# Full-row score products, and first-group weight conversion on one buffer without GpSimd, in an attention, expert and dense kernel

## The chip, the cores and the metric

One NeuronCore of a Trainium2 chip runs the whole program in one launch. The metric is device microseconds of that core, the median of several executions. A second number is the span, from the first to the last instruction of one profiled execution.

## The reference, cut to what matters

Three layers run one after the other, all in fp32.

```
scores = q @ k^T / 8, causal; a = softmax(scores); local = a @ v         # B, H, S, D = 4, 8, 576, 64
q_p = phi(q);  mem = (q_p @ M_prev) / (q_p . z_prev + 1e-6)
x = g * mem + (1 - g) * local                                            # 2304 tokens x 512
e = argmax(x @ w_gate);  x = gate * eom * relu(x @ w1[e]) @ w2[e]        # 8 experts, 1024 wide
h = relu(x @ w_in);  out = (h * h) @ w_out                               # dense, 2048 wide, weights given as float64
```

## The kernel before, in words

An fp32 product is made of three fp32r products (`mm3`): each operand is split into a high part that fp32r holds exactly and the rest, and high x high, high x low and low x high are summed in PSUM.

**Attention.** The 32 heads are worked as 16 pairs; the two heads of a pair lie on partitions 0 to 63 and 64 to 127. Each pair goes through four stages (prep, front, back, end), and in one round of the loop four neighbouring pairs are each in another stage; `PLAN` says how their steps are interleaved, and a scheduler at compile time then fixes the order of every engine's queue. In prep, ScalarE and VectorE split q and k into `qh`, `ql`, `kh`, `kl`, and SyncE (SP) issues eight DMAs that stack `kh` over `kl` and `qh` twice (`k2`, `q2`, L201 and L202), so that one product over 128 rows gives high x high and high x low of one head. In front, `scores` makes for each head the stacked product, then the product `ql` x `kh` over the 64 rows of this head alone (L229 both), and then a bf16 product that adds the causal mask (L239); the three calls cover 512, 256 + 128 and 384 columns. The last 64 query rows go another way (`psl`, full rows). In back, the weights are transposed into `aT` and multiplied with v (L332): four blocks of 128 key rows, and a fifth block of only 64 rows. v and the k and q of later pairs are loaded by SP as well; the load of v (L209) is the first DMA of a round in SP's queue and waits for the product of an earlier pair that read the same buffer.

**Experts.** Routed tokens run through their expert, in an order of ScalarE's, VectorE's, GpSimd's and TensorE's instructions that is written out by hand. Into this order two of the dense weight conversions (f = 0 and 1) and the first y transposes are put (`dense_prep`, `AH`).

**Dense.** Five groups of up to 512 tokens; each runs over 16 slices f of the hidden width: `l1` (12 products, L81 to L83 on `phf`), relu, square, split into `gT`, then `l2` (12 products on `po`), one f behind `l1`. During the first group the weights of slice f + 2 are converted from float64, whose bits are put together again with integer operations: for each of the two matrices (512 columns each) ScalarE takes the absolute value (L1089), VectorE runs four operations (L1091, L1093, L1096, L1098), ScalarE copies the high part (L1100) and GpSimd subtracts for the low part (L1102). GpSimd also makes the low part of `gT` in this group (L1168); in the others VectorE does. The later groups find the weights converted.

Of the kernel before, what the change touches and what calls it, by code (L numbers as in the profile page):

```python
# [33 lines left out]
GW = P + 32  # L34
NRAW = 3
AH = ((3, 0), (3, 2), (3, 2), (3, 2), (3, 2), (2, 0), (2, 2), (2, 2), (1, 1), (1, 1))
# [6 lines left out]
XG = 4  # L43
XF = 2
NP = 6
# [18 lines left out]
WARM = 11  # L64
MASK_LAST = True
TK = 3
# [69 lines left out]
def attention(tc, c, q, k, v, x_dram, pools):  # L136
# [9 lines left out]
    pvs = [lt.tile([P, SP_], F32, name=f"pvs{i}") if i else per.tile([P, SP_], F32, name=f"pvs{i}") for i in range(2)]  # L146
    qlast = [[per.tile([P, P], F32R, name=f"qlast{t}{i}") for t in "hl"] for i in range(2)]
    for i in range(3):
        nc.gpsimd.memset(qpad[i][:, S:], 0.0)
    for i in range(2):  # L150
        nc.gpsimd.memset(pvs[i][:, S:], 0.0)
        for t in range(2):
            nc.gpsimd.memset(qlast[i][t].bitcast(F32), 0.0)
    c.setup()
    c.lg = c.pool.tile([P, NCOL, 2 * E], F32, name="lg")
# [5 lines left out]
    def pair(b, hp, lgT):  # L161
# [18 lines left out]
        yield  # L180
        qh = fr.tile([P, S], F32R, tag="qh", name="qh")
        ql = fr.tile([P, S], F32R, tag="ql", name="ql")
        ex = fr.tile([P, S], F32, tag="ex", name="ex", bufs=1)
# [4 lines left out]
        nc.vector.scalar_tensor_tensor(out=ql, in0=qs, scalar=0.125, in1=qh.bitcast(F32), op0=ALU.mult, op1=ALU.subtract)  # L188
        for t, src in enumerate((qh, ql)):
            for h in range(2):  # L190
                r = slice(64 * h, 64 * h + 64)
                early.tensor_copy(qlast[i][t][r, r], src[r, 512:S].bitcast(F32))
# [14 lines left out]

        vt = ld.tile([P, NB, 2, D], F32, tag="vraw", name="vraw", bufs=2)
        nc.sync.dma_start(out=vt[:, 0:4].rearrange("p c h d -> p c (h d)"), in_=v[b, hp, 0:512].rearrange("(c p) d -> p c d", p=P))  # L209
# [7 lines left out]
        def scores(js):  # L217
            banks = [bank(f"sc{js[0]}{h}") for h in range(2)]
            off = [sum((i + 1) * P for i in js[:t]) for t in range(len(js))]
            o, n = off[-1] + js[-1] * P, len(js)  # L220
            mask = c.maskd.unsqueeze(1).to_broadcast((P, n, P))
            for h in range(2):
                r = slice(64 * h, 64 * h + 64)

                def product(qx, kx, start, stop):
                    for i, j in enumerate(js):
                        nk = (j + 1) * P
                        lhs, rhs = (qx[:, h], kx[:, h]) if len(qx.shape) == 3 else (qx[r], kx[r])
# [10 lines left out]
                nc.tensor.matmul(banks[h][:, o - (n - 1) * P:o + P], lhsT=c.identb, rhs=mask, start=False, stop=MASK_LAST)  # L239
                if not MASK_LAST:  # L240
                    product(ql, kh, False, True)
# [25 lines left out]

        aT = at.tile([P, 2, 1664], F32, tag="aT", name="aT", bufs=2)
        ko = (0, 576, 1024, 1344, 1536)
# [57 lines left out]
        for kb in range(NB):  # L327
            kn = P if kb < 4 else LAST
# [736 lines left out]
def dense_prep(tc, c, st, w_in, w_out):  # L1065
# [3 lines left out]
    cv = e(tc.tile_pool(name="cv", bufs=2, side="right", reuse_waits="tile"))  # L1069
    thr = 2.0 ** -15 * (1.0 + 0.125)  # L1070
    win32 = w_in.bitcast(I32).rearrange("(k p) (f t) -> p k f t", p=P, t=2)
# [4 lines left out]
    def weights(f, pool):  # L1076
        c.wi[f] = pool.tile([P, 2, 4, P], F32R, name=f"wi{f}")
        c.wo[f] = pool.tile([P, 2, DM], F32R, name=f"wo{f}")
        dst = [c.wi[f].rearrange("p t k f -> p t (k f)"), c.wo[f]]
        src = [win32[:, :, f * P:(f + 1) * P, :], wout32[f * P:(f + 1) * P]]  # L1080
        raw, u, x = ([cv.tile([P, 512] + [2] * (nm == "fraw"), dt, tag=nm, name=nm, bufs=nb) for _ in range(2)]
                     for nm, dt, nb in (("fraw", I32, NRAW), ("u", I32, 2), ("x", F32, XF)))
        for i in range(2):
            with tc.issue_after(c.last) if f < NPRE else nullcontext():
                nc.sync.dma_start(out=raw[i] if i else raw[i].rearrange("p (k f) t -> p k f t", k=4), in_=src[i])
        yield
        lw, hw = ([r[:, :, t] for r in raw] for t in range(2))
        for i in range(2):
            nc.scalar.activation(x[i], hw[i].bitcast(F32), AF.Abs)  # L1089
        for i in range(2):  # L1090
            nc.vector.tensor_scalar(out=u[i], in0=hw[i], scalar1=0x07FFFFFF, scalar2=3, op0=ALU.bitwise_and, op1=ALU.logical_shift_left)  # L1091
        for i in range(2):
            nc.vector.scalar_tensor_tensor(out=u[i], in0=lw[i], scalar=29, in1=u[i], op0=ALU.logical_shift_right, op1=ALU.bitwise_or)  # L1093
        yield
        for i in range(2):
            nc.vector.scalar_tensor_tensor(out=u[i], in0=hw[i], scalar=-1073741824, in1=u[i], op0=ALU.bitwise_and, op1=ALU.bitwise_or)  # L1096
        for i in range(2):
            nc.vector.scalar_tensor_tensor(out=x[i], in0=x[i], scalar=thr, in1=u[i].bitcast(F32), op0=ALU.is_ge, op1=ALU.mult)  # L1098
        for i in range(2):
            nc.scalar.copy(dst[i][:, 0], x[i])  # L1100
        for i in range(2):
            c.psub = nc.gpsimd.tensor_sub(dst[i][:, 1], x[i], dst[i][:, 0].bitcast(F32))  # L1102
        yield
# [3 lines left out]
    yT = c.yT[0] = c.yTeven()  # L1107
    yt = [cv.tile([P, 2, DM], F32, tag="fraw", name="ytp", bufs=NRAW) for _ in range(2)]
    for j in range(2):
        with tc.issue_after(c.last):  # L1110
            nc.sync.dma_start(out=yt[j], in_=c.y_first[2 * j * P:(2 * j + 2) * P].rearrange("(i p) f -> p i f", p=P))
    yield
    for j in range(4):
        turn(nc, c, c.bank("pty"), yt[j // 2][:, j % 2], yT[:, :, j])
        if j % 2:
            yield
# [13 lines left out]
def dense(tc, c, st, out):  # L1130
# [25 lines left out]
    def l1(g, f):  # L1156
# [20 lines left out]
    for g, (b0, nb) in enumerate(groups):  # L1177
# [23 lines left out]
        if g < len(groups) - 1:  # L1201
            l2(g, NF - 1, gts.pop(NF - 1), po, range(nb))
        else:
# [111 lines left out]
```

## Time and profile before

| | before |
|---|---|
| device time, median of 3 runs | 974.2 us (973.51 to 974.49) |
| the profiled execution's own time | 973.51 us |
| its span | 971.8 us |
| TensorE busy in the span | 930.1 us (96%) |
| VectorE, ScalarE, GpSimd busy | 599.5, 468.7, 246.4 us |
| mean granted clock of TensorE | 0.986 |

A busy TensorE is not one at its peak: the end of a matmul is modelled, and a start that is late because the array was not ready counts as busy too. What a product really costs is read from the distance between the starts of neighbours.

### The profile page before, as it was taken

Reading aid. Unit: us, or ns where it says so; the run is one execution under the profiler, and the core shown is the slowest. Engines: PE = TensorE matmul, PEld = TensorE weight load, DVE = VectorE, ACT = ScalarE, POOL = GpSimd, SP = SyncE. Lnnn points to the kernel's source line nnn. Section 1 sums busy time; section 2 is a strip of 40 time slices with the busy share of each in tenths; the row PEclk is TensorE's granted clock in tenths of the full one; section 3 lists DMA queues with packets and bytes.
Section 4 is the critical chain, followed back from the end, with each engine's and each line's share of the span. In section 5 each row is a group of like instructions: output and inputs, shape, how many; then the busy total and the mean of one; then the engine's idle time right before and its main releaser. Section 6 shows DMA issues by size and latency. Waiting matters only on the chain. (4 is left out here: it accounts for less than half of the span.)

```text
span 971.8 us, 14590 instructions
## 1 busy us (share of the span) xinstructions
PE 930.1 (96%) x5212; PEld 735.4 (76%) x5212; DVE 599.5 (62%) x1142; ACT 468.7 (48%) x950; POOL 246.4 (25%) x301
## 2 busy tenths in 40 slices
PE   7999999999999999999999787799999999999996
PEld 4676676776566889889898565678888888888895
DVE  6677878778486887767678899943223222322232
ACT  6877777774445666565563444442222222322231
POOL 6233233231201033054322555562001100100010
PEclk8999999999999999999999999899999999999999
DMA  9675575552746978765735444431000100100000
GB/s 194 168 173 144 145 174 147 131 136 84 236 140 209 377 263 306 258 230 198 272 111 166 136 132 131 130 87 65 12 11 33 33 1 0 44 1 1 12 33 22
DMA packets 80923, 125.03 MB, mean 129 GB/s; under 512 B 8848, under 2 KB 35472, under 8 KB 80848
## 3 DMA queue, kind: packets, MB, share of 16 engines
q1 hardware_dynamic: 76224, 109.11, 37.1%
q0 software_dynamic: 4624, 14.95, 4.8%
q8 instruction: 43, 0.70, 0.3%
q14 instruction: 32, 0.26, 0.1%
HBM read 109.10 MB, written 15.99 MB: 129 GB/s over the span
## 5 line engine op out<-in xcount | busy, mean ns | idle before, releaser
L1165 DVE SCALAR_TENSOR_TENSOR r<-phf,r 128x512 f32<-128x512 f32 (+1 forms) x80 | 50.9, 636 | 178.9 <-ACT r L1164 178.9
L81 PE MATMUL phf<-yT,wi 128*128 128x512 f32 (+1 forms) x320 | 123.3, 385 | 19.2 <-DVE r L1165 19.2
L1164 ACT ACTIVATE r<-phf 128x512 f32<-128x512 f32 (+1 forms) x80 | 44.4, 555 | 177.9 <-PE phf L83 163.0
L848 DVE TENSOR_TENSOR wc<-raw,wc 128x1024 fp32r<-128x1024 f32 x91 | 117.3, 1331 | 12.0 <-ACT wc L846 10.3
L83 PE MATMUL phf<-yT,wi 128*128 128x512 f32 (+1 forms) x320 | 120.1, 375 | 0.0
L82 PE MATMUL phf<-yT,wi 128*128 128x512 f32 (+1 forms) x320 | 119.9, 375 | 0.0
L846 ACT CAST wc<-raw 128x1024 fp32r<-128x1024 f32 x108 | 106.5, 1056 | 20.0 <-DMA raw<-in_w_dram 14.8
L81 PE MATMUL po<-wo,gT 128*128 128x512 f32 x256 | 101.6, 398 | 1.5 <-ACT gT L1167 1.5
L82 PE MATMUL po<-wo,gT 128*128 128x512 f32 x256 | 101.0, 395 | 0.0
L83 PE MATMUL po<-wo,gT 128*128 128x512 f32 x256 | 89.0, 390 | 0.0
L81 PEld LDWEIGHTS phf<-yT,wi 128*128 128x128 f32 x320 | 61.2, 191 | 35.6 <-DVE r L1165 18.6
L244 DVE TENSOR_REDUCE negm<-sc 128x1 f32<-128x512 f32 (+3 forms) x128 | 59.0, 483 | 30.6 <-PE sc L239 28.6
L247 ACT ACTIVATE a<-sc,negm 128x512 f32<-128x512 f32 (+3 forms) x128 | 67.1, 529 | 21.5 <-DVE negm L244 20.7
L81 PE MATMUL py<-wc,hT 128*128 128x512 f32 x176 | 69.9, 397 | 0.7 <-ACT hT L885 0.7
L82 PE MATMUL py<-wc,hT 128*128 128x512 f32 x176 | 68.8, 391 | 0.8 <-DVE wc L848 0.8
L83 PEld LDWEIGHTS phf<-yT,wi 128*128 128x128 f32 x320 | 61.3, 192 | 10.8
L83 PE MATMUL py<-wc,hT 128*128 128x512 f32 x176 | 68.9, 391 | 0.3 <-DVE hT L886 0.3
L82 PEld LDWEIGHTS phf<-yT,wi 128*128 128x128 f32 x320 | 61.5, 192 | 10.0
L848 POOL TENSOR_TENSOR wc<-raw,wc 128x1024 fp32r<-128x1024 f32 x17 | 45.2, 2658 | 91.6 <-ACT wc L846 83.9
L1212 POOL DMA_INDIRECT out_dram<-ob,rtok x13 | 12.9, 991 | 204.7 <-DVE ob L1211 179.6
L1167 ACT CAST gT<-r 128x512 fp32r<-128x512 f32 x64 | 39.8, 621 | 45.4 <-DVE r L1165 37.0
L81 PEld LDWEIGHTS po<-wo,gT 128*128 128x128 f32 x256 | 49.3, 193 | 12.9 <-ACT gT L1167 2.2
(338 smaller groups left out, 2092.5 us busy)
## 6 DMA issues: line engine op xcount, KB each, us to landing
raw<-in_w_dram SPq DMA_DIRECT2D x64, 1024.0 KB, 6.7
fraw<-in_w_in_dram SPq DMA_DIRECT2D x16, 512.0 KB, 4.0
fraw<-in_w_out_dram SPq DMA_DIRECT2D x16, 512.0 KB, 3.7
q<-qh SPq DMA_DIRECT2D x60, 128.0 KB, 2.5
kraw<-in_k_dram SPq DMA_DIRECT2D x16, 288.0 KB, 5.3
qraw<-in_q_dram SPq DMA_DIRECT2D x16, 288.0 KB, 3.2
y_rest<-y SPq DMA_DIRECT2D x17, 256.0 KB, 3.0
vraw<-in_v_dram SPq DMA_DIRECT2D x16, 256.0 KB, 3.1
```

Of the source, the lines that this page charges most:

```text
L81: nc.tensor.matmul(out, lhsT=lh, rhs=rh, start=start, stop=False)
L82: nc.tensor.matmul(out, lhsT=lh, rhs=rl, start=False, stop=False)
L83: return nc.tensor.matmul(out, lhsT=ll, rhs=rh, start=False, stop=stop)
L244: nc.vector.tensor_reduce(out=negm[:, h, j:j + 1], in_=psv, axis=AX.X, op=ALU.max, negate=True)
L247: nc.scalar.activation(a[:, h, aoff[j]:aoff[j] + nk], psv, AF.Exp, bias=negm[:, h, j:j + 1], accum_out=ssum[:, h, j:j + 1])
L846: nc.scalar.copy(wc[:, 0, ks], raw[:, ks])
L848: eng.tensor_sub(wc[:, 1, ks], raw[:, ks], wc[:, 0, ks].bitcast(F32))
L1164: nc.scalar.activation(r[:, 0:nt], ph[:, 0:nt], AF.Relu)
L1165: nc.vector.scalar_tensor_tensor(out=r[:, 0:nt], in0=ph[:, 0:nt], scalar=0.0, in1=r[:, 0:nt], op0=ALU.max, op1=ALU.mult)
L1167: nc.scalar.copy(gT[:, 0, 0:nt], r[:, 0:nt])
L1212: nc.gpsimd.indirect_dma_start(out=out, out_offset=bass.IndirectOffsetOnAxis(ap=c.tok[b0 + j], axis=0), in_=ob, in_offset=None)
```

## The change

It has two parts that do not touch each other.

In attention, `ql` x `kh` becomes a product over all 128 rows: `ql` is carried by two more DMAs into a buffer `qlz` whose other 64 rows are zero for each head, and the partner is `kh` of both heads. The fifth block of the product with v takes 128 rows too; the buffers of v and `aT` become permanent, with zeros in the rows that are not used. `qh` and `ql` have one buffer in place of two.

In the dense part, both matrices of a slice are converted by one operation of each kind over 1024 columns, in place in one buffer `x`: absolute value, a maximum with a small number, three integer operations, the copy of the high part, and the subtraction, now on VectorE. The square in the first group moves from VectorE to ScalarE, the low part of `gT` from GpSimd to VectorE, and `l2` runs two f behind `l1` in this group.

```diff
-NRAW = 3
+NRAW = 2
-XF = 2
+XF = 1
...
+    qlz = [per.tile([P, 2, 512], F32R, name=f"qlz{i}") for i in range(2)]
+    vts = [per.tile([P, NB, 2, D], F32, name=f"vts{i}") for i in range(2)]
+    aTs = [per.tile([P, 2, 1664], F32, name=f"aTs{i}") for i in range(2)]
...
+        for h in range(2):
+            nc.gpsimd.memset(qlz[i][64 - 64 * h:128 - 64 * h, h].bitcast(F32), 0.0)
+        nc.gpsimd.memset(vts[i][LAST:P, 4], 0.0)
+        nc.gpsimd.memset(aTs[i][LAST:P, :, 1536:1600], 0.0)
...
-        qh = fr.tile([P, S], F32R, tag="qh", name="qh")
-        ql = fr.tile([P, S], F32R, tag="ql", name="ql")
+        qh = fr.tile([P, S], F32R, tag="qh", name="qh", bufs=1)
+        ql = fr.tile([P, S], F32R, tag="ql", name="ql", bufs=1)
...
-        for t, src in enumerate((qh, ql)):
-            for h in range(2):
-                r = slice(64 * h, 64 * h + 64)
+        for h in range(2):
+            r = slice(64 * h, 64 * h + 64)
+            nc.sync.dma_start(out=qlz[i][r, h].bitcast(F32), in_=ql[r, 0:512].bitcast(F32))
+            for t, src in enumerate((qh, ql)):
                 early.tensor_copy(qlast[i][t][r, r], src[r, 512:S].bitcast(F32))
...
-                if MASK_LAST:
-                    product(ql, kh, False, False)
+                for i_, j in enumerate(js):
+                    nk = (j + 1) * P
+                    nc.tensor.matmul(banks[h][:, off[i_]:off[i_] + nk], lhsT=qlz[i][:, h, j * P:nk], rhs=kh[:, 0:nk], start=False, stop=False)
...
-                nc.tensor.matmul(pa[o, q0 - P:448], lhsT=vt[0:kn, kb, h, :], rhs=aT[0:kn, h, ko[kb] + q0 - kb * P:ko[kb] + S - kb * P],
+                nc.tensor.matmul(pa[o, q0 - P:448], lhsT=vt[:, kb, h, :], rhs=aT[:, h, ko[kb] + q0 - kb * P:ko[kb] + S - kb * P],
...
+        raw = cv.tile([P, 2, 512, 2], I32, tag="fraw", name="fraw", bufs=NRAW)
+        x = cv.tile([P, 1024], I32, tag="x", name="x", bufs=XF)
+        xf = x.bitcast(F32)
...
+        nc.scalar.activation(xf, hw.bitcast(F32), AF.Abs)
+        nc.vector.tensor_scalar_max(xf, xf, tiny)
+        nc.vector.tensor_scalar(out=x, in0=x, scalar1=0x07FFFFFF, scalar2=3, op0=ALU.bitwise_and, op1=ALU.logical_shift_left)
+        nc.vector.scalar_tensor_tensor(out=x, in0=lw, scalar=29, in1=x, op0=ALU.logical_shift_right, op1=ALU.bitwise_or)
+        nc.vector.scalar_tensor_tensor(out=x, in0=hw, scalar=-1073741824, in1=x, op0=ALU.bitwise_and, op1=ALU.bitwise_or)
+        nc.scalar.copy(hi, xf)
         yield
...
-            c.psub = nc.gpsimd.tensor_sub(dst[i][:, 1], x[i], dst[i][:, 0].bitcast(F32))
+        c.psub = nc.vector.tensor_sub(lo, xf, hi.bitcast(F32))
...
-        nc.vector.scalar_tensor_tensor(out=r[:, 0:nt], in0=ph[:, 0:nt], scalar=0.0, in1=r[:, 0:nt], op0=ALU.max, op1=ALU.mult)
-        gT = dg.tile([P, 2, 512], F32R, tag="gT", name="gT", bufs=2) if g < len(groups) - 1 else c.gring[:, f % 8]
+        if g:
+            nc.vector.scalar_tensor_tensor(out=r[:, 0:nt], in0=ph[:, 0:nt], scalar=0.0, in1=r[:, 0:nt], op0=ALU.max, op1=ALU.mult)
+        else:
+            nc.scalar.activation(r[:, 0:nt], r[:, 0:nt], AF.Square)
+        gT = dg.tile([P, 2, 512], F32R, tag="gT", name="gT", bufs=3) if g < len(groups) - 1 else c.gring[:, f % 8]
...
-        (nc.vector if g else nc.gpsimd).tensor_sub(gT[:, 1, 0:nt], r[:, 0:nt], gT[:, 0, 0:nt].bitcast(F32))
+        nc.vector.tensor_sub(gT[:, 1, 0:nt], r[:, 0:nt], gT[:, 0, 0:nt].bitcast(F32))
...
+        lag = 1 if g else 2
...
-                if f >= 1:
-                    l2(g, f - 1, gts.pop(f - 1), po, range(nb))
+                if f >= lag:
+                    l2(g, f - lag, gts.pop(f - lag), po, range(nb))
```

## Rows read from the trace of the kernel before

**Rows 1.** Busy time in two stretches: length, each engine's us, TensorE clock, DMA share.

```profile
50.00:200.00 150.00, 150.00 (x1109) 107.00 (x1108) 116.58 (x329) 112.44 (x324) 47.58 (x96) 1.00 0.62 153
...
600.00:610.00 10.00, 6.12 (x25) 4.81 (x26) 10.00 (x13) 4.59 (x8) 5.31 (x4) 0.97 0.49 149
```

**Rows 2.** TensorE in order of time, one round of attention: start us, us, instruction.

```profile
108.36 0.29 PE L82 MATMUL psl<-kl,qlasth 128*128 128x288 f32 x1
108.49 0.29 PE L83 MATMUL psl<-kh,qlastl 128*128 128x288 f32 x1
...
110.19 0.49 PE L229 MATMUL sc<-kh,ql 64*128 64x512 f32 x1
110.61 0.23 PE L239 MATMUL sc<-maskd,identb 128*128 128x128 bf16 x1
110.65 0.48 PE L229 MATMUL sc<-k,q 128*128 128x512 f32 x1
111.06 0.50 PE L229 MATMUL sc<-kh,ql 64*128 64x512 f32 x1
```

**Rows 3.** Weight loads by form, 50 to 200 us: count, busy, mean ns, idle before.

```profile
L229 PEld LDWEIGHTS sc<-k,q 128*128 128x128 f32 x82 | 14.3, 193 | 0.7 <-issue 0.3
L229 PEld LDWEIGHTS sc<-kh,ql 64*128 64x128 f32 x82 | 13.6, 183 | 10.8 <-issue 9.2
...
L239 PEld LDWEIGHTS <-identb 128*128 128x128 bf16 x62 | 5.9, 95 | 10.3 <-issue 8.7
...
L332 PEld LDWEIGHTS pva<-aT,vraw 64*64 64x64 f32 x40 | 2.3, 131 | 2.5 <-issue 2.5
```

**Rows 4.** SP's queue in order of time, one round.

```profile
105.09 0.38 SPq L209 DMA_DIRECT2D vraw<-in_v_dram  x1
...
114.86 0.45 SPq L170 DMA_DIRECT2D kraw<-in_k_dram  x1
120.55 0.38 SPq L209 DMA_DIRECT2D vraw<-in_v_dram  x1
```

**Rows 5.** The start: GpSimd and TensorE in order of time.

```profile
6.65 0.41 POOL L156 MEMSET lg<- 128x320 f32 x1
...
11.77 0.23 PE L239 MATMUL sc<-maskd,identb 128*128 128x128 bf16 x1
17.85 1.11 PE L77 MATMUL ptl<-ident,al 128*128 128x128 f32 x4 [5.86 <-ACT al L257]
```

**Rows 6.** VectorE in order of time, first dense group, f = 2 and f = 11.

```profile
552.61 0.68 DVE L1165 SCALAR_TENSOR_TENSOR r<-phf,r 128x512 f32<-128x512 f32 x1
...
624.88 0.68 DVE L1165 SCALAR_TENSOR_TENSOR r<-phf,r 128x512 f32<-128x512 f32 x1
```

**Rows 7.** Single lines: ns shortest/median/longest, first and last start us, form.

```profile
L1091 DVE TENSOR_SCALAR u<-fraw x32: 411/417/1515, 499.3 to 632.1; 128x512 int32<-128x512 int32 x32
L1093 DVE SCALAR_TENSOR_TENSOR u<-fraw,u x32: 676/679/1785, 500.6 to 633.0; 128x512 int32<-128x512 int32 x32
L848 DVE TENSOR_TENSOR wc<-raw,wc x91: 1204/1217/3435, 261.5 to 516.1; 128x1024 fp32r<-128x1024 f32 x91
L846 ACT CAST wc<-raw x108: 1029/1054/1098, 260.4 to 515.6; 128x1024 fp32r<-128x1024 f32 x108
L1102 POOL TENSOR_TENSOR wo<-x,wo x16: 1277/1348/1747, 509.2 to 639.6; 128x512 fp32r<-128x512 f32 x16
```

**Rows 8.** A later dense group in order of time: TensorE, ScalarE, VectorE.

```profile
802.40 0.39 PE L81 MATMUL phf<-yT,wi 128*128 128x512 f32 x1
...
805.12 0.39 PE L81 MATMUL phf<-yT,wi 128*128 128x512 f32 x1
...
804.64 0.60 ACT L1164 ACTIVATE r<-phf 128x512 f32<-128x512 f32 x1 [3.62 <-PE phf L83]
...
805.27 0.69 DVE L1165 SCALAR_TENSOR_TENSOR r<-phf,r 128x512 f32<-128x512 f32 x1 [3.52 <-ACT r L1164]
```

**Rows 9.** Both ends of the first dense group in order of time: ScalarE, TensorE.

```profile
536.58 0.61 ACT L1100 CAST wi<-x 128x512 fp32r<-128x512 f32 x1
...
639.78 0.50 PE L81 MATMUL phf<-yT,wi 128*128 128x512 f32 x1
```

More of the change, by code (lines that the diff above doesn't have):

```diff
@@ L64 @@
 WARM = 11
-MASK_LAST = True
 TK = 3
@@ L206, in pair @@
         yield "prep"
-        vt = ld.tile([P, NB, 2, D], F32, tag="vraw", name="vraw", bufs=2)
+        vt = vts[i]
         nc.sync.dma_start(out=vt[:, 0:4].rearrange("p c h d -> p c (h d)"), in_=v[b, hp, 0:512].rearrange("(c p) d -> p c d", p=P))
@@ L236, in scores @@
                     product(qh, kl, False, False)
-                if MASK_LAST:
-                    product(ql, kh, False, False)
-                nc.tensor.matmul(banks[h][:, o - (n - 1) * P:o + P], lhsT=c.identb, rhs=mask, start=False, stop=MASK_LAST)
-                if not MASK_LAST:
-                    product(ql, kh, False, True)
+                for i_, j in enumerate(js):
+                    nk = (j + 1) * P
+                    nc.tensor.matmul(banks[h][:, off[i_]:off[i_] + nk], lhsT=qlz[i][:, h, j * P:nk], rhs=kh[:, 0:nk], start=False, stop=False)
+                nc.tensor.matmul(banks[h][:, o - (n - 1) * P:o + P], lhsT=c.identb, rhs=mask, start=False, stop=True)
             views = [(banks[h][:, off[i]:off[i] + (j + 1) * P], h, j) for i, j in enumerate(js) for h in range(2)]
@@ L266, in pair @@
         yield "front"
-        aT = at.tile([P, 2, 1664], F32, tag="aT", name="aT", bufs=2)
+        aT = aTs[i]
         ko = (0, 576, 1024, 1344, 1536)
@@ L327, in pair @@
         for kb in range(NB):
-            kn = P if kb < 4 else LAST
             q0 = max(P, kb * P)
@@ L1069, in dense_prep @@
     cv = e(tc.tile_pool(name="cv", bufs=2, side="right", reuse_waits="tile"))
-    thr = 2.0 ** -15 * (1.0 + 0.125)
+    tiny = 2.0 ** -15
     win32 = w_in.bitcast(I32).rearrange("(k p) (f t) -> p k f t", p=P, t=2)
@@ L1076, in weights @@
     def weights(f, pool):
[L1077 to L1082, printed above, removed]
@@ L1083, in weights @@
-        for i in range(2):
-            with tc.issue_after(c.last) if f < NPRE else nullcontext():
-                nc.sync.dma_start(out=raw[i] if i else raw[i].rearrange("p (k f) t -> p k f t", k=4), in_=src[i])
-        yield
[L1087 to L1091, printed above, removed]
@@ L1092, in weights @@
-        for i in range(2):
-            nc.vector.scalar_tensor_tensor(out=u[i], in0=lw[i], scalar=29, in1=u[i], op0=ALU.logical_shift_right, op1=ALU.bitwise_or)
-        yield
[L1095 to L1100, printed above, removed]
@@ L1101, in weights @@
-        for i in range(2):
-            c.psub = nc.gpsimd.tensor_sub(dst[i][:, 1], x[i], dst[i][:, 0].bitcast(F32))
+        w = pool.tile([P, 2, 2, 512], F32R, name=f"w{f}")
+        c.wi[f] = w[:, :, 0].rearrange("p t (k q) -> p t k q", k=4)
+        c.wo[f] = w[:, :, 1]
+        hi, lo = (w[:, t].rearrange("p i q -> p (i q)") for t in range(2))
+        raw = cv.tile([P, 2, 512, 2], I32, tag="fraw", name="fraw", bufs=NRAW)
+        x = cv.tile([P, 1024], I32, tag="x", name="x", bufs=XF)
+        xf = x.bitcast(F32)
@@ new lines, in weights @@
+        with tc.issue_after(c.last) if f < NPRE else nullcontext():
+            nc.sync.dma_start(out=raw[:, 0].rearrange("p (k f) t -> p k f t", k=4), in_=win32[:, :, f * P:(f + 1) * P, :])
+            nc.sync.dma_start(out=raw[:, 1], in_=wout32[f * P:(f + 1) * P])
+        yield
+        lw, hw = (raw.rearrange("p i q t -> p (i q) t")[:, :, t] for t in range(2))
+        nc.scalar.activation(xf, hw.bitcast(F32), AF.Abs)
+        nc.vector.tensor_scalar_max(xf, xf, tiny)
+        nc.vector.tensor_scalar(out=x, in0=x, scalar1=0x07FFFFFF, scalar2=3, op0=ALU.bitwise_and, op1=ALU.logical_shift_left)
@@ L1107, in dense_prep @@
     yT = c.yT[0] = c.yTeven()
-    yt = [cv.tile([P, 2, DM], F32, tag="fraw", name="ytp", bufs=NRAW) for _ in range(2)]
+    yt = cv.tile([P, 4, DM], F32, tag="fraw", name="ytp", bufs=NRAW)
     for j in range(2):
         with tc.issue_after(c.last):
-            nc.sync.dma_start(out=yt[j], in_=c.y_first[2 * j * P:(2 * j + 2) * P].rearrange("(i p) f -> p i f", p=P))
+            nc.sync.dma_start(out=yt[:, 2 * j:2 * j + 2], in_=c.y_first[2 * j * P:(2 * j + 2) * P].rearrange("(i p) f -> p i f", p=P))
     yield
     for j in range(4):
-        turn(nc, c, c.bank("pty"), yt[j // 2][:, j % 2], yT[:, :, j])
+        turn(nc, c, c.bank("pty"), yt[:, j], yT[:, :, j])
         if j % 2:
@@ L1201, in dense @@
         if g < len(groups) - 1:
-            l2(g, NF - 1, gts.pop(NF - 1), po, range(nb))
+            for f in sorted(gts):
+                l2(g, f, gts.pop(f), po, range(nb))
         else:
```

## The prediction, made before the changed kernel was run

> **What bounds the kernel now.** I read the stretches first, then the order of each queue inside them. In attention TensorE is busy for all 150 of 150 us, with VectorE at 116.6, ScalarE at 112.4 and DMA at 0.62 [rows 1]: nothing but TensorE sets the pace there. The reader should then ask whether TensorE streams or waits inside its busy time, and the distances between starts answer. Two full-row fp32r products of 288 columns stand 0.13 us apart, which is 0.45 ns a column, so 512 columns should take 0.23 us. The 64-row product of 512 columns holds the mask behind it up for 0.42 us (110.19 to 110.61), and the full-row product ahead of a 64-row one holds that up for 0.41 (110.65 to 111.06); but from the mask, full rows, to the next full-row product it is 0.04 [rows 2]. So each change between 64 and 128 rows costs about 0.19 us. The weight loads say the same in another way: those of the 64-row products sit idle for 10.8 us, those of the mask behind them for 10.3, those of the 64-row block of the product with v for 2.5, while those of the full-row products of the same line sit idle for 0.7 [rows 3].
>
> In the first dense group TensorE has only 6.1 of 10 us and VectorE has all 10 [rows 1]. A slice takes 8.03 us there (552.61 to 624.88 for nine) [rows 6], against 2 x 2.72 = 5.44 us of TensorE's work (twelve starts from 802.40 to 805.12 in a later group) [rows 8]. VectorE is full because its operations are stretched: the same form takes 0.41 or 1.5 us, 0.68 or 1.8 [rows 7], and GpSimd subtracts beside it all the time.
>
> **Attention, product by product.** The 82 weight loads of stacked products [rows 3] are 8 a pair, so 10.25 pairs pass in 150 us and a round is 14.6 us. The idle time of the three groups that the change turns into full rows, 10.8 + 10.3 + 2.5 = 23.6 us, is 2.3 us a pair; the starts give the same (12 changes of form in the scores at 0.19). Columns streamed stay as they are, so TensorE's round falls to 12.3 us. What is late next? VectorE has 116.6 / 10.25 = 11.4 us in a round, ScalarE 11.0. SP issues its 16 DMAs from 105.09 to 115.3, 0.64 us each, and then waits for the next round [rows 4]; with the two for `qlz` it needs 11.5 us. DMA would go from 0.62 to about 0.78, with 0.26 MB more on 2.2 MB in a round and less time for it. With four queues between 11 and 12.3 us, each in fixed order, I take 12.9 us a round: 1.7 us over 15 rounds, **25 us less**. The bounds are 34 us (all of TensorE's saving) and 10 us (a round of 13.9, if SP or VectorE hold it).
>
> The added wait on SP is for `ql`; behind it stand the stacking DMAs of a pair whose scores come a round later, so the slack of that round covers it. Without that cover the pair's scores wait for it, 1.3 us a round for the two issues. The single buffers of `qh` and `ql` make the next pair's split wait for this pair's DMAs, issued a round earlier: hidden for the same reason. A permanent buffer for v and `aT` changes nothing in their number.
>
> The Trainium skill, page TensorEngine Tiling (Array Packing), section When to Use Tiling, speaks against this part: with a contraction of 64 or less it wants two row tiles that work side by side. By it the full-row form would give up half of the two heads' streaming, 1280 columns or some 0.6 us a pair, 9 us in all. The trace does not bear it out here: the two 64-row products of a call start 0.87 us apart, with a mask and a stacked product between them, so there is no overlap to lose [rows 2].
>
> **The start.** GpSimd must clear four pieces of 512 columns and four small ones ahead of the masks. A clear of 320 columns takes 0.41 us [rows 5], so this is up to 4 us; and the first pair's `ql` product now waits for two DMAs among the first loads. Behind the first scores TensorE has a gap of 5.9 us anyway, until 17.85 [rows 5], which covers some of it. Bounds 0 and 6; I take **3 us more**.
>
> **The two conversions among the experts.** In the written order ScalarE's copy of the high part now stands right behind the absolute value and waits for four operations of VectorE, 0.68 + 0.68 + 1.21 + 1.21 = 3.8 us (prices below), twice; behind it wait casts of expert weights, then their subtractions, then TensorE. The weights are taken two chunks ahead, which covers most of it. Bounds 0 and 7.6; I take **1.5 us more**.
>
> **The first dense group.** GpSimd's work goes away, and with it the stretching, so prices are the short ones of rows 7. On 1024 columns a two-operand operation of VectorE takes 1.21 us; a cast of ScalarE 1.05, and the absolute value is priced as a cast. The one-operand operations of VectorE are not shown at this size: between 0.42 (512 columns) and 1.21; as 512 columns more cost a two-operand operation 0.54 and these run at half the price a column (0.42 against 0.68 at 512), I take 0.42 + 0.27 = 0.68. VectorE's work then fits. But there is only one buffer `x`, and everything happens in place: absolute value, maximum, shift, or, or, copy, subtraction, and only then the next slice's absolute value. That is a chain of 1.05 + 0.68 + 0.68 + 1.21 + 1.21 + 1.05 + 1.22 = 7.1 us, and seven hand-overs at 0.03 (ScalarE ends at 805.24, VectorE starts at 805.27) [rows 8] make it **7.3 us a slice**: still more than TensorE's 5.44, and not far from 8.03. ScalarE's relu, square and cast and VectorE's low part of `gT`, 2.5 us a slice, share these queues; they fit into the chain's pauses, but not always, and I add 0.4.
>
> The ends: the first copy into the dense weights can run at 536.6 as before [rows 9], so slice 2 is ready at 538.9 and slice 15 after 13 x 7.7 us, at 639.0; GpSimd's last subtraction ends at 641.0 now [rows 7]. Then TensorE still has `l1` of slice 15 and `l2` of 14 and 15, 8.2 us, and is through at 647.2. Now it runs without a gap from 639.78 on [rows 9] with five such halves left, 13.6 us, to 653.4. That is **6 us less**. Without any blocking it is 11 less; with all 2.5 us in the chain (9.8 a slice) it is 21 more; 8.2 a slice changes nothing. The later `l2` hides the making of `gT` and is worth nothing while the weights are late.
>
> The square on ScalarE is no loss: 0.60 us for a pass there against 0.69 on VectorE, the fuller engine [rows 8]. The Trainium skill, page ScalarE: Activation LUTs, section Rules for kernel authors, would put such plain arithmetic on VectorE. By it 0.6 us a slice would stand in VectorE's queue again, at worst 13 x 0.6 = 8 us in the chain; for fp32 at this size the trace shows no advantage of VectorE.
>
> **Sum.** -25 + 3 + 1.5 - 6 = -26.5 us from the profiled execution's own 973.5 gives 947.0; the median lies 0.7 above that execution, so **948 us**. A measurement of this kernel can tell 0.2%, 2 us, from no change.
>
> **Rivals.**
> - Another queue takes the round over: SP's 18 issues with a wait, or VectorE, hold it near 13.9 us. For it: 11.5 us of issuing in a round leave SP under 1 us beside the wait at its head [rows 4]. Against it: that wait is for TensorE, which is itself faster. Attention gives 10 us: -10 + 4.5 - 6, about 963. Chance 0.18.
> - Slower: the conversion chain. If TensorE's order puts an `l2` ahead of the `l1` whose weights have just come, ScalarE's relu, square and cast stand ahead of the copy and hold it by 2.7 us (one half of TensorE), so a slice takes about 10. Then slice 15 is ready at 668.9 and the group ends at 677, 24 us later: -25 + 4.5 + 24, about 978. It decides from 9.7 us a slice on. For it: ScalarE runs in order and there is one buffer. Against it: ScalarE's three passes fit while VectorE has its 3.8 us. Chance 0.08.
> - The pauses of rows 3 do not come from the rows of the product, and stay: 974.2 + 4.5 - 6, about 973. Against it: only neighbours of 64-row products show them, the same line with full rows does not. Chance 0.05.
> - Better than the sum: rounds near 12.4 us and an unblocked chain give 934 or less. Chance 0.05.
>
> The forecast keeps 0.64, and its own range is 938 to 957. The range that should hold eight in ten reaches into the first rival and to most of TensorE's saving: 932 to 966. Faster: 0.64 + 0.18 + 0.05 and a little of the third rival, 0.88; same 0.04; slower 0.08.
>
> **What the profile after would show.** All score products with 128 rows, 0.23 us from start to start at 512 columns, and weight loads of `qlz` and the mask with next to no idle time. Attention's last scores some 20 us earlier; TensorE busy for less than all of it, with the releaser of its gaps naming the next queue. In the first dense group no operation of VectorE at 1.5 us or more, one conversion each 7.3 to 8.2 us, and ScalarE's absolute value waiting for VectorE's subtraction. The prediction is wrong if TensorE's distances stay at 0.4 us, if a round stays above 13.9 us, or if a slice takes over 9.7.

## The result and the profile after

The change takes the kernel from 973.9 us (973.5 to 974.5) to 949.3 us (946.7 to 951.9, 4 runs): a ratio of 0.9747, 95% interval 0.9719 to 0.9775, 24.6 us less. The profiled execution took 951.9 us itself, its span is 950.2 us, its mean granted clock 0.986. In the trace the first product of the experts starts at 227.7 us where it started at 250.2, so 22.5 us come from attention with its start. The rest gives almost nothing: from the first dense relu to the last, 421.0 us before have become 420.7.

The busy time by stretches, with the columns of [rows 1]:

```profile
50.00:200.00 150.00, 149.36 (x1243) 115.41 (x1243) 138.64 (x377) 121.83 (x365) 53.54 (x102) 1.00 0.75 185
600.00:610.00 10.00, 8.90 (x39) 7.03 (x38) 7.28 (x10) 5.07 (x6) 0.00 (x0) 1.00 0.34 116
```

In attention TensorE is still busy all the time, with 12% more products in the same 150 us; VectorE has risen from 116.6 to 138.6 us. In the first dense group VectorE is no longer full and GpSimd has nothing to do, but no engine has taken its place: the stretch has no full queue.

One round of attention on TensorE, in order of time, answers to [rows 2]:

```profile
100.59 0.48 PE L236 MATMUL sc<-k,q 128*128 128x512 f32 x1
100.91 0.40 PE L246 MATMUL sc<-kh,qlz 128*128 128x512 f32 x1
101.15 0.23 PE L247 MATMUL sc<-maskd,identb 128*128 128x128 bf16 x1
101.19 0.47 PE L236 MATMUL sc<-k,q 128*128 128x512 f32 x1
```

The stacked product now holds the low product up for 0.32 us (it was 0.41), and that one holds the mask up for 0.24 (it was 0.42); the next low product, not shown, starts at 101.50. The weight loads by form between 50 and 200 us answer to [rows 3]:

```profile
L236 PEld LDWEIGHTS sc<-k,q 128*128 128x128 f32 x93 | 16.1, 194 | 1.1 <-issue 0.3
...
L246 PEld LDWEIGHTS sc<-kh,qlz 128*128 128x128 f32 x93 | 15.8, 191 | 0.0
L247 PEld LDWEIGHTS <-identb 128*128 128x128 bf16 x70 | 6.7, 96 | 9.7 <-issue 9.7
```

The idle time of the low product is gone, that of the mask is not. 93 loads in 150 us are 11.6 pairs, a round of 12.9 us. (By a mark that each pair leaves once, the score reduction shown further down, four pairs take 52.2 us, from 65.30 to 117.51, which is 13.05 a round.)

Single lines of the converted slices between 515 and 625 us, with the columns of [rows 7], and the subtraction on VectorE that ends the conversions of f = 3 and f = 15, in order of time, which answers to [rows 6]:

```profile
L1096 DVE TENSOR_SCALAR x<-x x13: 691/695/737, 519.6 to 617.6; 128x1024 int32<-128x1024 int32 x13
L1098 DVE SCALAR_TENSOR_TENSOR x<-fraw,x x13: 1214/1224/1226, 522.1 to 619.6; 128x1024 int32<-128x1024 int32 x13
L1099 ACT CAST w<-x x14: 1028/1044/1052, 515.3 to 620.9; 128x1024 fp32r<-128x1024 f32 x14
L1101 DVE TENSOR_TENSOR w<-x,w x14: 1224/1225/1262, 516.4 to 622.0; 128x1024 fp32r<-128x1024 f32 x14
```

```profile
524.47 1.23 DVE L1101 TENSOR_TENSOR w<-x,w 128x1024 fp32r<-128x1024 f32 x1 [1.16 <-ACT w L1099]
...
621.97 1.22 DVE L1101 TENSOR_TENSOR w<-x,w 128x1024 fp32r<-128x1024 f32 x1 [1.11 <-ACT w L1099]
```

The stretched operations are gone, shortest and longest agree. But the twelve slices between those two subtractions take 97.5 us, 8.12 each, where a slice of before took 8.03. One of the long ones, 9.4 us, shows why; ScalarE, VectorE and TensorE in order of time:

```profile
565.59 1.17 ACT L1094 ACTIVATE x<-fraw 128x1024 f32<-128x1024 f32 x1 [0.77 <-DVE w L1101]
570.82 0.60 ACT L1163 ACTIVATE r<-phf 128x512 f32<-128x512 f32 x1 [4.06 <-PE phf L82]
571.45 0.63 ACT L1167 ACTIVATE r<-r 128x512 f32<-128x512 f32 x1
572.12 0.62 ACT L1169 CAST gT<-r 128x512 fp32r<-128x512 f32 x1
572.64 1.04 ACT L1099 CAST w<-x 128x1024 fp32r<-128x1024 f32 x1
...
569.51 1.22 DVE L1098 SCALAR_TENSOR_TENSOR x<-fraw,x 128x1024 int32<-128x1024 int32 x1
573.72 1.23 DVE L1101 TENSOR_TENSOR w<-x,w 128x1024 fp32r<-128x1024 f32 x1 [0.26 <-ACT w L1099]
...
564.35 0.79 PE L80 MATMUL phf<-yT,w 128*128 128x512 f32 x1 [2.63 <-ACT w L1099]
...
565.37 0.63 PE L80 MATMUL po<-w,gT 128*128 128x512 f32 x1
565.80 0.63 PE L81 MATMUL po<-w,gT 128*128 128x512 f32 x1
...
570.40 0.39 PE L82 MATMUL phf<-yT,w 128*128 128x512 f32 x1
```

VectorE has the integer word ready at 570.73, and ScalarE copies it only at 572.64: relu, square and cast of the layer, 1.82 us, stand ahead. They come so late because TensorE, after a pause of 2.63 us, ran its products 0.43 us apart instead of 0.23: the stretch 564 to 566 us shows a granted clock of 0.60, so for most of it the lower of the two levels (1.2 of 2.4 GHz).

### The profile page after: what moved, and what is told of

Its sections match the earlier page's. It is cut to its first block, busy times and chain, and to the rows that moved or that the text cites. A ratio compares the mean times of both kernels' runs of the same rounds, so it can differ in the third digit from the quotient of the medians.

```text
span 950.2 us, 14491 instructions
## 1 busy us (share of the span) xinstructions
PE 906.1 (95%) x5212; PEld 730.1 (77%) x5212; DVE 582.8 (61%) x1094; ACT 468.8 (49%) x934; POOL 187.0 (20%) x261
## 5 line engine op out<-in xcount | busy, mean ns | idle before, releaser
L1165 DVE SCALAR_TENSOR_TENSOR r<-phf,r 128x512 f32<-128x512 f32 (+1 forms) x64 | 40.0, 624 | 175.5 <-ACT r L1163 175.5
L80 PE MATMUL phf<-yT,w 128*128 128x512 f32 (+1 forms) x320 | 120.4, 376 | 10.6 <-ACT w L1099 10.6
L81 PE MATMUL phf<-yT,w 128*128 128x512 f32 (+1 forms) x320 | 118.9, 372 | 0.0
L82 PE MATMUL phf<-yT,w 128*128 128x512 f32 (+1 forms) x320 | 118.8, 371 | 0.0
L80 PE MATMUL po<-w,gT 128*128 128x512 f32 x256 | 102.4, 402 | 11.3 <-ACT gT L1169 11.3
L81 PE MATMUL po<-w,gT 128*128 128x512 f32 x256 | 101.6, 397 | 0.0
L82 PE MATMUL po<-w,gT 128*128 128x512 f32 x256 | 91.7, 393 | 0.0
L80 PEld LDWEIGHTS phf<-yT,w 128*128 128x128 f32 x320 | 61.0, 191 | 24.4 <-ACT w L1099 13.0
L81 PEld LDWEIGHTS phf<-yT,w 128*128 128x128 f32 x320 | 61.0, 191 | 10.7
L82 PEld LDWEIGHTS phf<-yT,w 128*128 128x128 f32 x320 | 60.9, 190 | 10.5
L80 PEld LDWEIGHTS po<-w,gT 128*128 128x128 f32 x256 | 48.8, 191 | 25.3 <-ACT gT L1169 15.4
L1170 DVE TENSOR_TENSOR gT<-r,gT 128x512 fp32r<-128x512 f32 x64 | 44.3, 692 | 33.6 <-ACT gT L1169 33.4
L250 DVE TENSOR_REDUCE negm<-sc 128x1 f32<-128x512 f32 (+3 forms) x128 | 55.6, 477 | 7.6 <-PE sc L247 7.6
L81 PEld LDWEIGHTS po<-w,gT 128*128 128x128 f32 x256 | 49.1, 192 | 10.1
```

Of the source, the lines that this page charges most:

```text
L80: nc.tensor.matmul(out, lhsT=lh, rhs=rh, start=start, stop=False)
L81: nc.tensor.matmul(out, lhsT=lh, rhs=rl, start=False, stop=False)
L82: return nc.tensor.matmul(out, lhsT=ll, rhs=rh, start=False, stop=stop)
L1170: nc.vector.tensor_sub(gT[:, 1, 0:nt], r[:, 0:nt], gT[:, 0, 0:nt].bitcast(F32))
```

## The experiments

Times are medians, ratios are to the kernel before on the same chip, with their 95% intervals. Three groups of four ran on three chips, where the kernel before took 973.3 us (the two parts alone, the distance of one slice without and with a second buffer), 972.4 us (the changed kernel again, the 64 rows, no low product, the second buffer at a distance of two) and 972.7 us (the other four). Diffs are cut, and of a long line only the part that changes is shown.

### The two parts alone

The kernel before with only the attention edits (the first diff says what of the changed kernel is taken back), then with only the dense edits (the second).

```diff
-NRAW = 2
-XF = 1
+NRAW = 3
+XF = 2
...
-    tiny = 2.0 ** -15
+    thr = 2.0 ** -15 * (1.0 + 0.125)
```

```diff
-    qlz = [per.tile([P, 2, 512], F32R, name=f"qlz{i}") for i in range(2)]
...
-                lhsT=qlz[i][:, h, j * P:nk], rhs=kh[:, 0:nk]
+                    product(ql, kh, False, False)
```

> Only the attention edits on the kernel before; the dense part is as before. Theory: the marks of the two traces put 12 rounds of 1.8 us, 21 to 22 us, into the attention, and nothing comes back later; the dense group and its two early conversions, unchanged here, then cost what they cost before. Expected 974 - 22 = 952 us (950 to 954), the 16 wide score reductions at the times of the changed kernel within 1 us. Rival: the two parts help each other (the first dense group gains only because it starts at another time, or the attention is slowed by what the dense part prefetches); then this run and the next don't add up to the whole change, 24.6 us, and this one comes out under 945 or over 957.

> Only the dense edits on the kernel before; attention is as before. Theory from the marks of the two traces: the two conversions among the experts cost 1.7 us and the dense part gives 0.3 back, so 975.3 us (973.5 to 977), no gain at all. Rival, the prediction's own sum: 1.5 more among the experts and 6 less in the first dense group, 969.4 us. Either way VectorE shows no operation of 1.5 us or more in that group.

Attention alone: 950.1 us, ratio 0.9780 (0.9765 to 0.9796), 21.4 us less by the ratio and 23.2 by the medians. The dense part alone: 973.0 us, 0.9992 (0.9980 to 1.0003), nothing. Together they make the whole change within its interval. So, to within that interval, neither part helps the other, the prediction's 4.5 us from the dense part are not there, and the question is where they went.

### Rows of the low product

```diff
-  lhsT=qlz[i][:, h, j * P:nk], rhs=kh[:, 0:nk]
+  lhsT=qlz[i][r, h, j * P:nk], rhs=kh[r, 0:nk]
```

The DMAs, the zeros, the single buffers stay, and the order of the instructions on all five engines is that of the changed kernel, which ran beside it.

> The changed kernel itself, as a reference on the same chip as the runs beside it. Expected 949 us; both parts alone gave -21.4 and -0.3 of 1000 parts times 974, together about 951. If the two layers' distance in the first dense group is worth nothing, it lies within 2 us of the run with a distance of one, 951.1.

> The changed kernel with its zero-padded operand, its DMAs, its buffers and its place for the low product all kept, but the product reads only the 64 rows of its own head of both operands. Theory: the pauses come from the change between 64 and 128 rows; they come back, 1.6 to 1.8 us a pair by the distances of starts, so 20 to 24 us over 13 to 15 rounds, 970 to 974. Rival (the prediction's third): the pauses come from something else that the change moved, such as the product's place ahead of or behind another or the single buffers of qh and ql; then the time stays at 949 to 953 and TensorE's weight loads of this product show no idle time.

The changed kernel took 950.6 us, 0.9763 (0.9744 to 0.9781); with 64 rows it takes 969.0, 0.9956 (0.9940 to 0.9973): 18.4 us come back, a little less than expected. TensorE of this run in order of time:

```profile
108.64 0.48 PE L236 MATMUL sc<-k,q 128*128 128x512 f32 x1
109.05 0.49 PE L246 MATMUL sc<-kh,qlz 64*128 64x512 f32 x1
109.48 0.23 PE L247 MATMUL sc<-maskd,identb 128*128 128x128 bf16 x1
109.52 0.48 PE L236 MATMUL sc<-k,q 128*128 128x512 f32 x1
```

The distances 0.41 and 0.43 us are back with nothing else changed. So the number of rows makes the pauses, and the prediction's third rival falls. By starts 64 rows cost 0.28 us more for the 512 columns of a head, 0.28 for the 384 and 0.24 for the 256 and 128, 1.60 us a pair. The wide score reduction that each pair starts with (sixteen in all; here the fourth and the last, of the run with 64 rows and of the changed kernel beside it) shows how much of that reaches the round:

```profile
41.97 0.76 DVE L262 TENSOR_REDUCE negm<-psl 128x1 f32<-128x576 f32 x1
...
224.49 0.74 DVE L262 TENSOR_REDUCE negm<-psl 128x1 f32<-128x576 f32 x1
```

```profile
40.20 0.76 DVE L262 TENSOR_REDUCE negm<-psl 128x1 f32<-128x576 f32 x1
...
206.72 0.74 DVE L262 TENSOR_REDUCE negm<-psl 128x1 f32<-128x576 f32 x1
```

Twelve rounds take 182.5 and 166.5 us: 1.33 of the 1.60 us arrive in each.

### Rows of the last block with v

```diff
-  lhsT=vt[:, kb, h, :], rhs=aT[:, h, ...]
+  lhsT=vt[0:P if kb < 4 else LAST, kb, h, :], rhs=aT[0:P if kb < 4 else LAST, h, ...]
```

> The changed kernel, but the last block of the product with v reads its 64 rows only, as before the change; every queue keeps its order. Theory, that only the change of rows matters: 2.5 us of idle weight loads in 10.25 pairs, 0.24 us a pair, 16 pairs, come back: 950.6 + 3 to 4, so 953.5 to 954.5. Rival: the block hides behind work of other engines or its extra zero rows cost what the change of rows costs; then 950.6 within 1.5.

953.4 us, 0.9813 (0.9795 to 0.9831), against 0.9763 for the change: 3 to 5 us come back. The last wide reduction comes at 209.64 us, 2.9 later, and the weight loads of this block sit idle for 2.6 us again (44 of them). With the 18.4 of the low product that is all that attention gives.

### What holds the round now

First the low product left out, then kept at 64 columns.

```diff
-  for i_, j in enumerate(js):
-      ...
-      nc.tensor.matmul(banks[h][:, off[i_]:off[i_] + nk], lhsT=qlz[i][:, h, j * P:nk], rhs=kh[:, 0:nk], ...)
```

```diff
-  banks[h][:, off[i_]:off[i_] + nk], lhsT=qlz[i][:, h, j * P:nk], rhs=kh[:, 0:nk]
+  banks[h][:, off[i_]:off[i_] + 64], lhsT=qlz[i][:, h, j * P:nk], rhs=kh[:, 0:64]
```

> Leaves out part of the computation: the product of the low part of q with k for queries 0 to 511 (its DMAs, the split and all else stay). It asks what holds a round of attention at 12.9 us after the change. Theory, TensorE itself: its starts give 0.24 + 0.18 + 0.23 us for these products in each head, 1.3 us a pair, so up to 15 x 1.3 = 20 us less; VectorE has 11.9 us of work a round, which allows 1.0 a round, 15 us less. So 929 to 936. Rival, the prediction's step: VectorE, ScalarE, SP or DMA hold the round at 12.9; then 946 to 950, and TensorE shows idle time in attention that ends on one of them.

> Leaves out part of the computation: the product of the low part of q with k is made for 64 keys only, instead of up to 512; the number of products, DMAs and waits stays, so the order of the queues changes less than in the run that left the product out. TensorE has some 0.18 us less for each of the wide products, about 1.0 us a pair. Theory, TensorE sets the round of 12.9 us: 10 to 15 us less, 936 to 941. Rival, the prediction's step: the four queues together, each in a fixed order, hold it there: 948 to 952, with TensorE no longer busy all the time and no queue full.

Without the product: 955.9 us, 0.9820 (0.9796 to 0.9844), slower than with it. With 64 columns: 944.7 us, 0.9719 (0.9701 to 0.9737), some 4 us less. The busy time from 50 to 200 us, first without the product, then with 64 columns:

```profile
50.00:200.00 150.00, 139.53 (x1131) 107.51 (x1128) 129.94 (x353) 116.47 (x349) 54.63 (x101) 0.98 0.74 179
```

```profile
50.00:200.00 150.00, 146.77 (x1286) 118.38 (x1286) 137.85 (x396) 122.18 (x368) 54.48 (x102) 1.00 0.75 185
```

In both TensorE is no longer full, and no other engine is. With 64 columns the product's distance to what follows it falls by 0.21 us for the 512 columns, 0.15 for 384, 0.09 for 256 and 0.03 for 128, 0.96 a pair; the twelve rounds get 0.42 shorter each. (In this trace attention as a whole ends 8.9 us earlier than in the changed kernel beside it, by the first product of the experts, 219.18 against 228.09; 4.1 of these are there at the fourth wide reduction already, 36.09 against 40.20, where the order of the queues is another.) So TensorE alone doesn't set the round any more: less than half of what it is relieved of arrives. Neither run isolates what takes over, because the compile-time scheduler gave every queue another order: slightly with 64 columns, throughout without the product. Why the time got worse there is not shown; the other order is one candidate, another the granted clock, 0.98 in this stretch. Which wait comes next stays open.

### The start

```diff
-  nc.sync.dma_start(out=qlz[i][r, h], in_=ql[r, 0:512])
+  if b or hp:
+      nc.sync.dma_start(out=qlz[i][r, h], in_=ql[r, 0:512])
...
-  lhsT=qlz[i][:, h, j * P:nk], rhs=kh[:, 0:nk]
+  lhs, rhs = (qlz[i][:, h], kh) if b or hp else (ql[r], kh[r])
...
-        for h in range(2):
-            nc.gpsimd.memset(qlz[i][64 - 64 * h:128 - 64 * h, h].bitcast(F32), 0.0)
     c.setup()
+    for i in (1, 0):
+        for h in range(2):
+            nc.gpsimd.memset(qlz[i][64 - 64 * h:128 - 64 * h, h].bitcast(F32), 0.0)
...
```

The clears of `vts` and `aTs` move behind `c.setup()` too. This was made on the version with a second buffer `x` and a distance of two slices below.

> The kernel with a second buffer x and a distance of two, 928.8 us, with the start relieved: the first pair multiplies the 64 rows of the low part directly, with no DMA for the padded operand, and GpSimd clears the padded operands behind the masks instead of ahead of them. Theory: at the fourth wide reduction the start of the change costs about 2 us (41.97 against 40.05 us with the same 64-row products), and this gives them back: 926 to 927.5. Rival: the rounds behind the start absorb it, or the new order of the queues moves more than that: 928.8 within 1, or slower.

931.1 us, 0.9579 (0.9557 to 0.9601), against 928.8, 0.9549 (0.9530 to 0.9568): no gain. The first pair's low product does start earlier, at 7.28 us in place of 12.81. But the order of the queues is another, mainly in the first 45 us, and the fourth and the last wide reduction, first without this edit, then with it, come later:

```profile
39.93 0.76 DVE L262 TENSOR_REDUCE negm<-psl 128x1 f32<-128x576 f32 x1
...
206.07 0.74 DVE L262 TENSOR_REDUCE negm<-psl 128x1 f32<-128x576 f32 x1
```

```profile
42.78 0.74 DVE L266 TENSOR_REDUCE negm<-psl 128x1 f32<-128x576 f32 x1
...
209.30 0.74 DVE L266 TENSOR_REDUCE negm<-psl 128x1 f32<-128x576 f32 x1
```

So of the second theory the half on the order of the queues holds: 2.9 us are lost by the fourth reduction. The half on absorbing does not: 3.2 us are still there at the last. What the start of the change costs in the end, this run does not tell.

### The distance of the second layer, and a second buffer x

```diff
-  lag = 1 if g else 2
+  lag = 1
-  gT = dg.tile(..., bufs=3)
+  gT = dg.tile(..., bufs=2)
```

> The changed kernel with the second layer one slice behind the first in the first dense group, as before the change, and two buffers of gT instead of three. The prediction's theory: the conversion chain sets the pace, so the later second layer is worth nothing: 949 us within 2. Rival: with one slice of distance TensorE waits for the low part of gT, which stands behind the conversion's operations in VectorE's queue, so the next first layer, its relu and with it ScalarE's copy in the chain come later: a slice of 8.6 us or more instead of 8.1, 955 us or more.

```diff
-  x = cv.tile([P, 1024], I32, tag="x", name="x", bufs=XF)
+  x = (pool if f >= NPRE and f % 2 else cv).tile([P, 1024], I32, tag="x", name="x", bufs=XF)
```

> As the run with a distance of one slice, and every second slice converts in a second buffer x, so the absolute value need not wait for the subtraction of the slice before. Theory, the chain through the one buffer sets the pace: VectorE's 0.69 + 0.69 + 3 x 1.23 + 0.69 for gT = 5.8 us and TensorE's 5.44 us a slice are next, so a slice takes 6.0 to 6.6 us and the whole 20 to 27 us less than with one buffer: 922 to 930. Rival: the pace comes from waits on TensorE's order (relu late, copy behind it) or from the loads of the weights; then a slice stays above 7.6 us and the time within 6 us of the run with one buffer.

The same at a distance of two slices, with two buffers instead of three for the loads of y to make the room.

> The changed kernel with the second buffer x for every second slice and its distance of two slices kept (one buffer fewer for the loads of y makes the room). With one buffer x the distance was worth nothing. Theory: with two, TensorE has 9.5 of 10 us and waits 7.2 us for the parts of gT, so now the later second layer gives 3 to 6 us against the 929.9 of the run with a distance of one: 924 to 927. Rival: the loads of the weights, for which ScalarE waits 26 us, set the pace; then 930 within 2.

A distance of one slice: 951.1 us, 0.9769 (0.9751 to 0.9787), the same as the change. With the second buffer: 929.9 us, 0.9562 (0.9550 to 0.9575) at a distance of one and 928.8, 0.9549 (0.9530 to 0.9568) at two. One buffer more is worth 21 us, and the distance nothing in either case, against the theory of the third of these runs (924 to 927 us). The same two subtractions, f = 3 and f = 15, at a distance of one, and the chain of work that ended last:

```profile
524.48 1.22 DVE L1101 TENSOR_TENSOR w<-x,w 128x1024 fp32r<-128x1024 f32 x1
...
597.54 1.22 DVE L1101 TENSOR_TENSOR w<-x,w 128x1024 fp32r<-128x1024 f32 x1 [1.19 <-ACT w L1099]
```

```profile
PE 35%; DMA 5%; ACT 2%; issue 1%; DVE 1%; SPq 0%; POOLq 0%; ACTq 0%
```

A slice takes 6.09 us there, in place of 8.12. TensorE has 47.7 of 50 us between 545 and 595 us, and the loads of the weights (DMA, 5%) are what the chain has besides. So it was the serial chain through the one buffer that set the pace of the change.

### Where the square is made

```diff
-  if g:
+  if True:
       nc.vector.scalar_tensor_tensor(out=r[:, 0:nt], in0=ph[:, 0:nt], scalar=0.0, in1=r[:, 0:nt], op0=ALU.max, op1=ALU.mult)
```

> The changed kernel with the square of the first dense group on VectorE again, as before the change. Theory: VectorE's queue carries four of the chain's seven steps, so 0.69 us more in it for each slice lengthens the slice from 8.1 us to between 8.1 and 8.8: 950.6 + 0 to 9, most likely 954. Rival: ScalarE's relu, square and cast stand ahead of its copy of the high part, in the chain too, and taking 0.63 us from there shortens the slice to 7.5 to 7.8: 943 to 947.

943.7 us, 0.9708 (0.9691 to 0.9725) against 0.9763 (0.9744 to 0.9781) for the change: 5 to 7 us faster with the square back on VectorE. My theory fell, the rival holds. The whole chain of one slice, ScalarE and VectorE in order of time:

```profile
560.91 1.04 ACT L1099 CAST w<-x 128x1024 fp32r<-128x1024 f32 x1 [0.83 <-DVE x L1098]
561.87 0.62 ACT L1169 CAST gT<-r 128x512 fp32r<-128x512 f32 x1
563.25 1.13 ACT L1094 ACTIVATE x<-fraw 128x1024 f32<-128x1024 f32 x1 [0.77 <-DVE w L1101]
566.95 0.60 ACT L1163 ACTIVATE r<-phf 128x512 f32<-128x512 f32 x1 [2.57 <-PE phf L82]
568.39 1.04 ACT L1099 CAST w<-x 128x1024 fp32r<-128x1024 f32 x1 [0.84 <-DVE x L1098]
...
561.99 1.23 DVE L1101 TENSOR_TENSOR w<-x,w 128x1024 fp32r<-128x1024 f32 x1 [0.51 <-ACT w L1099]
...
564.42 0.69 DVE L1095 TENSOR_SCALAR x<-x 128x1024 f32<-128x1024 f32 x1 [0.60 <-ACT x L1094]
565.14 0.69 DVE L1096 TENSOR_SCALAR x<-x 128x1024 int32<-128x1024 int32 x1
565.87 1.23 DVE L1097 SCALAR_TENSOR_TENSOR x<-fraw,x 128x1024 int32<-128x1024 int32 x1
567.13 1.22 DVE L1098 SCALAR_TENSOR_TENSOR x<-fraw,x 128x1024 int32<-128x1024 int32 x1
568.27 0.68 DVE L1165 SCALAR_TENSOR_TENSOR r<-phf,r 128x512 f32<-128x512 f32 x1
```

From copy to copy it is 7.48 us, and every slice from f = 7 on takes this to within 0.05 us: the copy waits for VectorE's word alone, and the layer's square is made on VectorE while that copy runs. The busy time of 545 to 605 us, first of this run, then of the change:

```profile
545.00:605.00 60.00, 46.56 (x194) 34.79 (x192) 50.24 (x57) 26.50 (x33) 0.00 (x0) 1.00 0.41 140
```

```profile
545.00:605.00 60.00, 46.58 (x174) 34.94 (x172) 42.60 (x45) 28.36 (x37) 0.00 (x0) 0.91 0.38 129
```

TensorE is busy for the same time in both, but does 194 operations in place of 174 in it: its granted clock is 1.00 and not 0.91.

How the edit works is less clear than that it works, because it takes two things away at once: the square ahead of the copy, and the stretches at the lower clock level. In the change there are three of these in the twelve slices from f = 3 to f = 15 (the column PEclk, 0.50):

```profile
565.00:567.00 2.00, 2.00 (x6) 1.60 (x5) 1.37 (x3) 1.17 (x1) 0.00 (x0) 0.50 1.05 380
582.00:584.00 2.00, 2.00 (x6) 1.56 (x5) 0.81 (x2) 1.13 (x1) 0.00 (x0) 0.50 1.07 391
592.00:594.00 2.00, 2.00 (x6) 1.51 (x6) 1.93 (x3) 0.00 (x0) 0.00 (x0) 0.50 0.10 39
```

The slices that hold them take 9.38, 8.03 and 9.44 us. The first of the twelve, in which VectorE also has 1.28 us for the transposed y ahead of the last integer operation, takes 9.03. The other eight take 7.70 on average. With the square on VectorE no such stretch is left in the group, and of the 6.6 us that the twelve slices gain, 4.4 lie in those three. Whether the place of the square brings the falls of the clock about, and what it would cost without them, was not tested apart.

A second buffer and the square on VectorE were not run together. VectorE already has 45.1 of 50 us with the second buffer, so what that would give is open.

## Why the prediction came out, step by step

The sum was 947.0 us for one execution and 948 for the median; the median is 949.3 (the profiled execution lies 2.6 over it). That the median is only 1.3 us off is in part luck: like for like, the profiled execution took 951.9 us, 4.9 more than its sum, and the changed kernel run again had a median of 950.6, 21.8 us below the kernel before on that chip. Attention and the start together are right to half a microsecond, partly for a wrong reason; the conversions among the experts to about one; the first dense group is wrong.

- **Attention and start, -25 + 3 = -22: measured -22.5.** The mechanism, that a change between 64 and 128 rows stops TensorE, is shown by the run with 64 rows. TensorE's saving was mis-sized: the sum took the idle time of three groups of weight loads, 2.3 us a pair [rows 3]. Of the mask's 10.3 us 9.7 are still there after the change; a bf16 load behind an fp32r product is late in this view without delaying a product. The second sum, twelve changes at 0.19 us, overshoots too: with 64 rows the low product starts 0.09 us later behind the stacked one, and what follows it 0.05 to 0.20 later, by its width. By starts the saving is 1.60 us for the scores, and 2.9 us in all, 0.2 a pair, for the block with v: 1.8. The step after it, that the next queues hold the round at 12.9 us, erred the other way. TensorE still has 149.4 of 150 us, and most of its saving arrived, 1.33 of 1.60. The two errors cancelled, which is luck: the round is 12.9 us by the weight loads, 13.05 by the wide reductions.
- **The start, +3.** With the low product at 64 rows in the changed kernel the fourth wide reduction comes at 41.97 us; in the kernel before, with the same rows, it came at 40.05. So at this mark the start costs 1.9 us, inside the bounds. One mark later nothing of it is left (54.66 against 55.09 us), and in the changed kernel itself the fourth reduction comes at 40.05, no later than before. What the 3 us stand for in the end stays open: the run that was to relieve the start delayed it by 2.9 us, and that delay was not absorbed.
- **Conversions among the experts, +1.5.** From the first expert product to the last, 279.9 us became 281.6 in the profiled execution, but there TensorE has a granted clock of 0.50 from 268 to 270 us, behind a pause of 1.49 us. In the second profile of the changed kernel the granted clock is 1.00 there, behind a pause of 1.47, and the time is 280.1 us, in the run of the dense part alone 280.6. Without the fall of the clock the cost is 0.2 to 0.7 us. So more is hidden than the prediction allowed for; that the weights taken two chunks ahead hide it, as it says, was not tested.
- **First dense group, -6: measured nothing.** The chain through one buffer is there as worked out: the second buffer takes 2.0 us from a slice, and the operation that the trace did not show (one operand, 1024 columns) takes 0.69 us where 0.68 was estimated. The step that failed is "The square on ScalarE is no loss". It compared two durations, 0.60 and 0.69 us, and looked for the fuller engine; but the square's place in the order counts. On ScalarE it stands between relu and cast, ahead of the copy that is a link of the chain, and with it the blocking is 0.8 us a slice where the sum had 0.4. A slice of 8.12 us then gives nothing, as the sum itself says of 8.2. This excess is not spread evenly: eight of twelve slices take the forecast 7.70 us, and the rest is in the three with the granted clock at 0.50 and in the one with the transposed y, for neither of which the sum had a term. With the square on VectorE a slice takes 7.57 us on average (7.7 were forecast for the whole slice), and the group gives the 6 us forecast, to within about one. The Trainium skill, page ScalarE: Activation LUTs, section Rules for kernel authors, would have left it on VectorE, where it puts plain arithmetic such as max and mul for its speed in bf16. The run agrees (943.7 against 950.6 us), but not for speed: the pass takes 0.63 us on ScalarE and 0.68 on VectorE.
- **The later second layer "is worth nothing while the weights are late"**: shown, 951.1 against 950.6 us. With the weights early it was worth nothing either.
- **The rivals.** The slower one, relu, square and cast ahead of the copy, was the right mechanism at a smaller price: 1.9 us in a slice of 9.4 us, one of two of that length, not 2.7 in all. SP or VectorE holding the round at 13.9 did not come; that a next limit is near is shown by the run with 64 columns. The Trainium skill, page TensorEngine Tiling (Array Packing), section When to Use Tiling, spoke for row tiles of 64; with the two heads' products apart, as they stand here, full rows are 18.4 us faster, so the measurement decides against it in this place. No run here puts the two 64-row products side by side.

## What to carry to other kernels

Read what a switch of form costs from the distance between starts on TensorE; idle time of weight loads is only a hint of it, and a part of it can be free. Where a stage runs through one buffer in place, write its steps out as a chain over the engines and ask of every other operation on those engines whether it can stand ahead of a link: here its place in the queue counted, and neither its duration nor how full the engine was told of it. And before anything is made cheaper in such a chain, give it a second buffer: here that was worth as much as the whole change to attention.

## What was not expected of the hardware

The clock took part in the loss of the first dense group. Between 545 and 605 us TensorE is busy for 46.6 us in both of two kernels, in one with regular pauses of 1.65 to 1.74 us and a granted clock of 1.00, in the other with pauses of 1.1 to 2.6 us at irregular distances and 0.91. The fall at 564 us came behind the longest of them, 2.63 us. So a wait of TensorE was followed there by products 0.43 us apart, which made the next relu late and with it the next weights. The length of the pause alone does not tell when this happens: pauses of 2.00 us that end at 548.2 and 555.9 us were followed by no fall, one of 2.00 that ends at 580.5 was. Nor did the change bring it: the kernel before has five such stretches in this group, the granted clock at 0.50 at 555, 576, 586, 610 and 627 us.

The first fp32r product of 512 columns behind the transposes (100.59) or the bf16 mask (101.19) holds the next one up for 0.32 and 0.31 us, while the second takes 0.24, all at 128 rows. This 0.08 us stayed after the change and was part of the pauses that the prediction put down to the rows.
